# Cosformer attention followed by a leaky-ReLU feed-forward block on one core: a second order of the same steps, with other engines and ring places

## The chip, the cores and the metric

One core of a Trainium2 chip runs the program in one launch. The metric is the device time of one execution in microseconds (us). Five engines work side by side: TensorE (PE, with its weight loads as PEld), VectorE (DVE), ScalarE (ACT), GpSimd (POOL) and SyncE (SP), which here issues nearly all DMAs. Each engine runs its own instructions strictly in their order; between engines there are semaphores.

## The reference

```
r = max(x, 0); phi(x) = concat([r * cos_w, r * sin_w])         # head_dim 64 -> 128 features
kv  = einsum('bhsf,bhsd->bhfd', phi(k), v)                     # b 8, h 8, s 576, d 64
num = einsum('bhsf,bhfd->bhsd', phi(q), kv)
den = einsum('bhsf,bhf->bhs', phi(q), sum_s phi(k)) + 1e-6
x   = (num / den), heads side by side: 4608 tokens x 512
h   = x @ w_in                                                 # 512 x 2048
out = max(0.01 * h, h) @ w_out                                 # 2048 x 512, float32
```

All inputs and the output are float32 in DRAM; the matrix work is done in float16 with float32 sums.

## The kernel before, in words

The tokens are cut into nine groups of 512: groups 0 to 7 are the first 512 positions of the eight batches, group 8 gathers the 64 last positions of all eight. A group g passes through two halves.

**Attention half.** `lq`, `lk`, `lv` load q, k and v of a batch (L234, L244; L251 for group 8's q). `rq` and `rk` take the ReLU and round to float16 (L385 on ACT, L387 elsewhere). `kt` multiplies k by cosine or sine (L395, DVE), `v` copies v to float16, `kv` makes 72 small matmuls that contract over 64 rows (L444), `ko` copies their sums out. `q` multiplies q by cosine or sine (L408 ACT, L410 POOL, L414 DVE). `qT` turns two of a group's four q tiles by a DMA transposition on SP (L488). `n g.j` multiplies the turned q tile j with kv (8 matmuls, L544), `N g.j` divides (three DVE instructions, L555, L559, L560) and writes x. When all four are there, `xT g` turns the whole x of the group by one DMA transposition on SP (L500).

**Feed-forward half.** Groups 0 and 1 do it plainly (`f` L624, `e` L633, group 0's `F` L647 and store L662). From group 2 on, the first product is a 2x2 block scheme with seven products instead of eight (`f g.u.n`, four matmuls of 128x256 each, L763; u counts four column blocks). It needs sums of blocks of x, `X g.1` to `X g.4` (L677). The products are combined in four PSUM banks that are used in turn: `b`, `s` and `u` copy a bank on ACT or DVE (L420, L422), `y` and `z` add on DVE (L677), and `a`, `c`, `e`, `d` apply the leaky ReLU on ACT (L787). The second product is made the same way from group 1 on: `S g.n` are sums of blocks of the activations (L677, DVE), `F g.n.tt.h` the products (four matmuls of 128x256 each, L846), `M` and `O` take the sums out of PSUM, `D` stores them (L904 and L909; L895 for the last pieces). `W` and `T` make the sums of the weights once (L677). `cw` and `w` cast the weights as they arrive, and `i` are idle matmuls on a tile of zeros (L295) that fill the time before there is work.

**What sets the order.** No scheduler does: a string `ORDER` (from L31) names every step once, and the loop below emits them in this order. A step may carry the engine that does it (`:D` DVE, `:A` ACT, `:P` POOL) and the place in a ring of buffers that it takes (`@0` to `@3`). What a step is, is the same in both kernels; a step's instructions go to the end of their engine's queue, so the string fixes each engine's order, and a step that waits holds up everything behind it on its engine.

```
    for token in ORDER.split():
        token, *places[:] = token.split("@")
        name, _, e = token.partition(":")
        f, args = steps.pop(name)
        f(*args, *([engines[e]] if e else []))
```

A transposition is one DMA instruction on SP:

```
    def x_transpose_dma(g):
        nc.sync.dma_start_transpose(
            out=xT_tile(g).rearrange("p j c t -> p (j c) t"),
            in_=st["xs", g].rearrange("p j h d -> p (j h d)"),
        )
```

Of the kernel before, what the change touches and what calls it, by code (L numbers as in the profile page):

```python
# [37 lines left out]
xo0.1.0:A f0.1.c f0.2.c f0.3.a f0.1.b f0.3.c N0.1.1 cw.2:P cw.3:P xo0.0.1:D Lw1.5 f0.0.b xt0.1.1@0
f0.0.d f0.2.d f0.3.d f0.0.c Lw1.7 Lw1.8 xo0.1.1:D f0.3.e f0.4.a f0.0.e f0.2.e e0.1 cw.4:D f0.4.d
f0.1.d f0.1.e cw.8:D cw.5:D f0.5.a f0.5.d Lw1.6 Lq1@3 rq1.1:D rq1.0:D cw.7:P e0.0 f0.6.a@0 f0.6.d  # L40
f0.7.a q1.3.0:D q1.1.1:D f0.7.d Lw2.0@2 e0.2 q1.0.0:D q1.2.1:D q1.0.1:D q1.2.0:D w0.0:D Lk1.0 w0.2:D
cw.6:P e0.3 Lw2.1@1 q1.3.1:P f0.12@1 w1.0:P f0.13 rk1.0:D W1.1:D W0.1:D f0.14@0 f0.15 kt1.0.0 e0.6
f0.8@1 f0.9 e0.7 f0.10@0 f0.11 q1.1.0:A e0.4 qt1.3@1 qo1.3:A e0.5 F0.2.0 F0.3.0 F0.0.0@0 F0.3.2
qt1.2@1 F0.2.2 F0.1.0@1 F0.0.2 qt1.0@0 qo1.2:D qt1.1@1 w1.2:A Lv1.0 Lk1.1 v1.0:P qo1.0:D qo1.1:D
kt1.0.1 F0.0.4 F0.1.2 F0.0.6 F0.3.4 F0.3.6 kv1.0@1 F0.1.4 rk1.1:A kt1.1.0 F0.1.6 Lw2.2@0 Lw2.3.0
w2.0:D ko1.0:A n1.1.0@1 F0.2.4 F0.2.6 kt1.1.1 w2.2:A w3.0:A N1.1.0 F0.2.8 F0.3.8 n1.0.0@0 N1.0.0
F0.0.8 F0.3.10 F0.3.12 Lw2.3.2 w3.2:D F0.0.10 F0.2.10 F0.2.12 xt1.0.0@0 F0.2.14 Lv1.1 v1.1:A kv1.1@1
ko1.1:A lq2@3 rq2.0:P rq2.1:A F0.3.14 T1 q2.0.1:P q2.3.0:P O0.2:D@0 lk2@1 lv2.0@2 F0.0.12 n1.0.1@1
q2.2.1:P F0.0.14 O0.0:A@3 O0.3:D@1 n1.1.1 F0.1.8 F0.1.10 N1.0.1 xt1.1.0@1 xt1.0.1@0 F0.1.12 N1.1.1
xo1.0.1:D xo1.0.0:A q2.2.0:A q2.1.1:A F0.1.14 xo1.1.0:D xt1.1.1@0 q2.1.0:D q2.0.0:D xo1.1.1:A f1.4.0  # L50
f1.0.0@1 f1.1.0 f1.1.2 f1.5.0 f1.0.2 rk2.1:A v2.0:A f1.5.2 rk2.0:P kt2.0.0 kt2.1.1 kt2.0.1 q2.3.1:A
f1.4.2 f1.2.0@0 e1.0 e1.2 lv2.1 f1.3.0 W0.2:D kt2.1.0 T2 T3 f1.3.2 f1.2.2 T4 lk3@0 v2.1:P W0.4:D
f1.10@1 kv2 f1.11 e1.1 f1.6@0 rk3.1:A ko2:A qT2.0 e1.5 rk3.0:A n2.0 f1.7 N2.0 qT2.1 f1.12@1 kt3.0.0
f1.13 n2.1 lq3@2 e1.3 f1.8@0 rq3.1:P f1.9 lv3.0@3 O0.1:A@2 lv3.1 kt3.1.0 N2.1 e1.6 n2.2 f1.14@1
kt3.1.1 e1.4 N2.2 f1.15 rq3.0:A e1.7 n2.3 F1.1.0.0@0 F1.2.0.0@1 lq4@1 D0.1 kt3.0.1 N2.3 F1.2.1.0
F1.1.1.0 S1.1a S1.1b F1.1.1.1 F1.2.0.1 q3.2.0:D S1.1c F1.1.0.1 S1.2a F1.2.1.1 v3.0:A q3.1.0:A
q3.3.1:P q3.0.1:P q3.2.1:P v3.1:A kv3 M1.1:A S1.2b S1.2c F1.6.0.0@0 F1.6.1.0 F1.6.1.1 q3.3.0:A
q3.1.1:D S1.3c F1.6.0.1 O1.2@2 F1.5.0.0@1 xT2 S1.3a W0.3:D X2.1:D f2.0.1 S1.4b X2.2:D X2.3:D
F1.5.0.1 F1.5.1.0 f2.0.5 q3.0.0:A rq4.0:A ko3:A b2.0:A s2.0:A f2.0.6 M1.6 X2.4:P S1.3b f2.0.2 f2.1.1
D0.2 qT3.1 qT3.0 u2.0:D f2.0.3 F1.7.0.0 f2.0.7 rq4.1:A a2.0 z2.0 e2.0 F1.7.1.0 F1.7.1.1 f2.1.5 y2.0  # L60
b2.1:A S1.4a q4.0.0:A s2.1:A q4.1.0:D lv4.0@2 lv4.1 lk4@3 q4.2.1:P f2.0.4 c2.0 F1.5.1.1 n3.0 f2.1.6
D0.3 D1.2 q4.3.0:P q4.0.1:P D0.0 u2.1:A q4.1.1:A d2.0 f2.1.2 W1.2:P F1.7.0.1 f2.1.3 a2.1 W1.4:P
W1.3:P N3.0 lq5@0 f2.1.7 n3.1 f2.2.1 v4.1:P rk4.0:P M1.7 z2.1 F1.4.1.0 F1.4.0.0 rk4.1:P y2.1 f2.2.5
f2.1.4 e2.1 b2.2:A c2.1 f2.2.2 s2.2:A N3.1 n3.2 f2.2.6 q4.3.1:A d2.1 u2.2:A O1.5@0 v4.0:A f2.2.3
F1.3.1.0 F1.3.1.1 f2.2.7 N3.2 z2.2 n3.3 f2.3.1 F1.4.1.1 F1.4.0.1 F1.3.0.0 N3.3 y2.2 O1.4@1 e2.2
kt4.0.0 kt4.0.1 kt4.1.0 b2.3:A q4.2.0:A F1.3.0.1 f2.3.6 F2.1.0.0@0 a2.2 f2.3.5 u2.3:A c2.2 s2.3:A
f2.3.7 f2.2.4 F2.1.1.0 d2.2 f2.3.2 f2.3.3 y2.3 c2.3 a2.3 xT3 kt4.1.1 S2.1a z2.3 O1.3@2 qT4.0 X3.1:P
X3.2:P f2.3.4 d2.3 e2.3 kv4 f3.0.1 b3.0:A f3.0.5 F2.1.0.1 F2.1.1.1 f3.0.6 X3.3:D S2.1b S2.3b f3.0.2
M2.1:A ko4:A s3.0:D F2.2.0.0 f3.0.3 f3.1.1 n4.0 u3.0:A f3.0.7 F2.2.0.1 F2.2.1.0 F2.2.1.1 a3.0 S2.2a
S2.1c S2.3c S2.2c z3.0 e3.0 F2.6.0.0@1 b3.1:A rq5.1:A F2.6.1.0 f3.1.6 f3.1.2 N4.0 O2.2:D@3 S2.2b  # L70
y3.0 n4.1 u3.1:A lk5@2 rk5.0:P F2.6.1.1 f3.1.5 rq5.0:P q5.0.1:P q5.0.0:A X3.4:P qT4.1 D1.3 lv5.0@1
c3.0 rk5.1:A s3.1:A F2.5.0.0@0 f3.1.7 F2.5.1.0 F2.6.0.1 f3.0.4 N4.1 kt5.0.0 f3.1.3 D1.5 D2.2 lq6@3
# [6 lines left out]
f3.3.4 e3.3 O2.4@3 lk6@2 F2.3.1.1 b4.0:A f4.0.6 f4.0.2 N5.0 n5.1 F3.1.0.0@1 D2.5 s4.0:A c3.3 d3.3
q6.0.1:D q6.0.0:D S3.1b F3.1.1.0 F3.1.1.1 f4.0.3 u4.0:A O2.3@0 X4.3:D S3.2b f4.0.7 lq7@0 a4.0 S3.1c  # L80
f4.1.5 f4.1.1 F3.1.0.1 F3.6.0.0@0 N5.1 z4.0 D2.4 rk6.0:A e4.0 F3.6.1.0 S3.3c S3.2c b4.1:A qT5.1
F3.6.0.1 F3.6.1.1 f4.1.2 rq7.0:P q6.2.0:P q6.2.1:P rq7.1:P q6.3.0:P y4.0 M3.1:D X4.4:D n5.2 f4.1.6
F3.2.1.0 F3.2.1.1 rk6.1:A q6.1.1:A s4.1:A a4.1 u4.1:A c4.0 q6.3.1:A f4.1.3 f4.0.4 f4.1.7 F3.2.0.0
N5.2 M3.6 S3.3b z4.1 y4.1 d4.0 lv6.0@1 n5.3 F3.2.0.1 f4.2.1 F3.7.1.0 F3.7.0.0 F3.7.0.1 f4.2.5
F3.7.1.1 e4.1 b4.2:A N5.3 O3.2:A@3 kt6.0.0 kt6.1.1 v6.0:D kt6.0.1 D2.3 s4.2:A f4.2.6 f4.1.4 lv6.1
c4.1 qT6.0 f4.2.3 F3.5.0.0@1 F3.5.1.0 f4.2.2 v6.1:A u4.2:A M3.7 F3.5.0.1 f4.2.7 z4.2 d4.1 a4.2 e4.2
S3.4b y4.2 F3.4.0.0 f4.3.5 s4.3:D lq8.1@3 rq8.1:P xT5 f4.3.1 X5.1:P q7.0.1:P q7.0.0:A b4.3:A
F3.5.1.1 kt6.1.0 S3.4a F3.4.1.0 F3.4.1.1 f4.2.4 f4.3.6 f4.3.3 F3.4.0.1 f4.3.2 qT6.1 D3.2 d4.2 c4.2
u4.3:A a4.3 q7.1.1:A O3.5@0 q7.3.1:D z4.3 X5.2:P kv6 F3.3.1.0 f5.0.1 f4.3.7 f5.0.5 F3.3.0.0 lk7@2
O3.4@2 X5.3:D S4.1a y4.3 S4.3a e4.3 ko6:A n6.0 f4.3.4 b5.0:A f5.0.6 F4.1.0.0@0 D3.5 F4.1.1.0 lv7.0@1  # L90
# [1026 lines left out]
```

## Time and profile before

| what | value |
|---|---|
| time, three runs | 277.46 us median (276.22, 277.46, 277.86) |
| the profiled execution's own time | 278.54 us |
| its span, first to last instruction | 276.7 us, granted TensorE clock 0.994 |
| DMA traffic | 57.62 MB, HBM read 36.70 MB, written 9.44 MB |
| busy share of the 16 DMA queues' engines, 0 to 160 us | 0.90 to 1.12 in each 20 us |
| the same, 200 to 260 us | 0.23, 0.33, 0.12 |
| DMA transpositions on SP | 14 of q (median 5.1 us from issue to landing), 7 of x (5.0 us) |

The page of a profile gives each engine's busy time, and the chain of work that ended last. The view of waits names, for each engine, what ended its idle time. In a view in order of time a row has the start in us, the length in us, the engine (SPq is SP's sequencer while it issues a DMA), the line, what is written and read with the shapes, and in brackets the idle time before it with what ended it. Matmuls are pipelined: a group of four of 128x256 is shown 0.60 us long, but the next group starts 0.44 us after it.

### The profile page before, as it was taken

To read this page: it belongs to the slowest core of one execution; us is meant where nothing else is said; L and a number is where in the kernel's file an instruction comes from. 1 tells how busy PE (TensorE), PEld (TensorE's weight loads), DVE (VectorE), ACT (ScalarE), POOL (GpSimd) and SP (SyncE) were. 2 spreads that over 40 slices of the span, in tenths; PEclk is the share of its full clock that TensorE was granted. 3 is DMA by queue.
4 is the path that set the end of the run, shared out by engine and by line. 5 is a ranking of instruction groups with operands and counts; after the bars stand their busy time and mean duration, and the time that the engine had idled before them with its cause. 6 is when DMAs were issued, how large, how long until landed. Compare 5 with 4: busy or idle time off the path is not lost.

```text
span 276.7 us, 7179 instructions
## 1 busy us (share of the span) xinstructions
PE 263.6 (95%) x2942; PEld 222.3 (80%) x2942; DVE 222.0 (80%) x433; ACT 173.8 (63%) x278; POOL 81.4 (29%) x86
## 2 busy tenths in 40 slices
PE   8699999999989999997999999999999999999992
PEld 3366555555888999997999899999998999999981
DVE  4673797798989899999997899999688868867652
ACT  6645644898958977785787576665447636475300
...
GB/s 220 360 357 388 401 406 374 357 195 372 221 196 357 232 233 199 378 207 320 260 221 212 347 124 154 5 207 128 159 152 2 0 121 111 39 39 11 30 25 206
DMA packets 77265, 57.62 MB, mean 208 GB/s; under 512 B 49456, under 2 KB 65840, under 8 KB 76848
## 3 DMA queue, kind: packets, MB, share of 16 engines
...
q10 hardware_dynamic: 608, 0.52, 0.7%
q8 instruction: 23, 0.38, 0.6%
...
HBM read 36.70 MB, written 9.44 MB: 167 GB/s over the span
## 4 chain that ended last, share of the span: by engine, by line
PE 68%; DMA 14%; DVE 11%; issue 3%; SPq 1%; ACT 1%; POOL 1%; DVEq 0%; ACTq 0%
PE ps L846 27%; PE ps_f L763 26%; DMA qst<-in_q_dram 6%; PE ps_h L624 5%; DMA xT<-xs 5%; PE ps_o L647 4%; PE ps_kv L444 2%; PE ps_num L544 2%; DMA w1st<-in_moe_w_in_dram 2%; DVE qp L414 2%; DVE ext L677 1%; DMA out_dram<-osb 1%; DVE y L677 1%; DVE g L677 1%; DVE xs L560 1%
## 5 line engine op out<-in xcount | busy, mean ns | idle before, releaser
L787 ACT ACTIVATE g<-ps_f 128x512 f16<-128x512 f32 x84 | 48.9, 599 | 35.0 <-PE ps_f L763 20.2
L846 PEld LDWEIGHTS <-g 128*128 128x128 f16 x640 | 61.7, 98 | 6.5
L846 PE MATMUL ps<-w,g 128*128 128x256 f16 x496 | 65.3, 273 | 0.0
L763 PEld LDWEIGHTS <-w 128*128 128x128 f16 x448 | 48.7, 113 | 4.3 <-issue 3.5
L763 PE MATMUL ps_f<-xT,w 128*128 128x256 f16 x336 | 49.3, 273 | 2.2 <-DMA xT<-xs 2.2
L763 PEld LDWEIGHTS <-wext 128*128 128x128 f16 x336 | 36.7, 114 | 0.6
L846 PE MATMUL ps<-T,ext 128*128 128x256 f16 x240 | 32.6, 273 | 0.0
L624 PE MATMUL ps_h<-xT,w 128*128 128x512 f16 (+1 forms) x144 | 29.2, 356 | 0.2 <-ACT xT L420 0.2
L846 PEld LDWEIGHTS <-ext 128*128 128x128 f16 x256 | 24.8, 98 | 2.6
L763 PE MATMUL ps_f<-X,wext 128*128 128x256 f16 x176 | 26.3, 273 | 0.0
L624 PEld LDWEIGHTS <-w 128*128 128x128 f16 x144 | 15.7, 114 | 10.4
L677 DVE TENSOR_TENSOR ps_f<-ps_f,u 128x512 f32<-128x512 f32 x28 | 19.4, 694 | 4.8 <-PE ps_f L763 3.5
L677 DVE TENSOR_TENSOR y<-ps_f,s 128x512 f32<-128x512 f32 x28 | 19.1, 683 | 3.7 <-PE ps_f L763 3.5
L633 ACT ACTIVATE g<-ps_h 128x1024 f16<-128x1024 f32 x16 | 16.0, 1023 | 7.5 <-PE ps_h L624 7.3
L787 ACT ACTIVATE g<-y 128x512 f16<-128x512 f32 x28 | 17.8, 634 | 3.8 <-DVE y L677 3.8
L560 DVE TENSOR_TENSOR xs<-ps_num,rden 128x512 f16<-128x512 f32 x28 | 19.3, 691 | 1.0
L395 DVE TENSOR_TENSOR kp<-kst,ang 128x1152 f16<-128x1152 f16 x24 | 18.8, 805 | 0.7 <-ACT kst L385 0.7
L420 ACT COPY ps_f<-ps_f 128x512 f32<-128x512 f32 x25 | 14.3, 573 | 5.9 <-PE ps_f L763 5.3
L763 PE MATMUL ps_f<-X,w 128*128 128x256 f16 x112 | 16.9, 273 | 0.7 <-DVE y L677 0.4
L846 PE MATMUL ps<-ext,g 128*128 128x256 f16 x128 | 17.4, 273 | 0.0
L677 DVE TENSOR_TENSOR osb<-ps,ext 128x512 f32<-128x512 f32 x23 | 15.7, 682 | 2.0 <-PE ps L846 2.0
L763 PE MATMUL ps_f<-xT,wext 128*128 128x256 f16 x112 | 16.8, 272 | 0.0
...
## 6 DMA issues: line engine op xcount, KB each, us to landing
...
qst<-in_q_dram SPq DMA_DIRECT2D x7, 1024.0 KB, 10.6
...
```

The costliest lines, as they stand in the source:

```text
L395: nc.vector.tensor_tensor(out=st["kp", b][:, lo:hi, :, f * D : (f + 1) * D].rearrange("p c j (x y) -> p (c j) x y", y=2), in0=halved("k", ...
L414: eng.tensor_scalar(out=o, in0=i, scalar1=0.0, scalar2=col, op0=ALU.max, op1=ALU.mult)
L420: nc.scalar.copy(o, i)
L444: nc.tensor.matmul(ps[:, o, (c - lo) * NE : (c - lo + 1) * NE], lhsT=st["kp", b][sl, c, j, :], rhs=vm[sl, c, j, :], start=(j == 0), stop=( ...
L560: nc.vector.tensor_tensor(out=xs, in0=ps[:, :, 0 : 4 * NE].rearrange("p a (b e) -> p a b e", e=NE)[:, :, :, 0:D], in1=rden.rearrange("p (a ...
L624: nc.tensor.matmul(ps[:, m % 2, lo:hi], lhsT=w1[m // 4, c][0][:, w1[m // 4, c][1], m % 4 : 512 : 4], rhs=xT[:, lo // P : hi // P, c, :], s ...
L633: nc.scalar.activation(g_tile(g)[:, 2 * i : 2 * i + 2, :], st["h", g, i], AF.Lrelu)
L647: nc.tensor.matmul(st["ps_o", g, tt], lhsT=st["g", g][:, m, tt * P : (tt + 1) * P], rhs=w2[:, m, :], start=(m == 0), stop=(m == NFT - 1),)
L677: eng.tensor_tensor(out=o, in0=a, in1=b, op=op)
L763: nc.tensor.matmul(ps[:, mi * HT : (mi + 1) * HT], lhsT=a[:, c, 2 * r0 + mi : 512 : 4], rhs=b[:, c], start=(n in (1, 5) and mi == 0 and c ...
L787: nc.scalar.activation(g_tile(g)[:, m : m + 2, r * HT : (r + 1) * HT], {"a": A, "c": y22, "e": E, "d": B_}[e].rearrange("p (m t) -> p m t" ...
L846: nc.tensor.matmul(ps[:, tt], lhsT=a[:, i, tt * P : (tt + 1) * P], rhs=b[:, i], start=(first and i == 0), stop=(i == NPR - 1 and (apart or ...
```

## The change

Only the string `ORDER` is replaced. Every step that stood in it still stands in it once, so the number of matmuls (2942), of DMAs and of sums is the same. What differs is the order, the letter of the engine on some steps, and the ring places.

The string's first lines, a place around the transposition of x of group 4, and its end, of some 100 lines each:

```diff
-i.10@1 i.13@0 Lq0.0@3 rq0.0:A qt0.1.0@1 i.11@0 Lk0.0@0 Lq0.1 i.14@1 i.7@1 qt0.0.0@0 i.4@1 rq0.1:A
-qt0.0.1 rk0.0:P kt0.0.0 Lk0.3 kt0.0.1 rk0.3:D kt0.3.0 Lk0.1 rk0.1:D kt0.1.1 kt0.1.0 Lv0.0@1 i.6@1
...
-q5.3.1:D f3.3.3 kv5 F2.4.1.0 ko5:A d3.2 xT4 f3.3.6 F2.4.0.1 f3.3.2 n5.0 F2.4.1.1 rq6.0:P q5.3.0:P
-u3.3:A f3.3.7 z3.3 X4.1:D S3.2a f4.0.1 F2.3.0.0 F2.3.0.1 y3.3 q6.1.0:P X4.2:P a3.3 F2.3.1.0 f4.0.5
...
-F8.3.1.1 O8.5.0@0 F8.4.0.1 F8.4.1.1 O8.3.1@1 D8.5.1 O8.2:A@3 D8.2 D7.4 D7.3 F8.3.0.0 D8.3.1 D8.5.0
-F8.3.0.1 O8.4@2 D8.4 O8.3.0@3 D8.3.0
+Lk0.0@1 Lq0.0@2 i.14@0 rq0.0:P rk0.0:P qt0.0.0@1 qt0.1.0@0 i.12@0 qo0.0.0:A Lk0.2 kt0.0.0 kt0.0.1
+rk0.2:D i.3@1 i.5@1 i.2@1 Lq0.1 Lk0.1 qo0.1.0:A rq0.1:P rk0.1:A i.7@1 Lk0.3 Lv0.0@0 qt0.0.1 i.1@0
...
+kt5.1.1 lq6@1 u3.3:A c3.2 f3.3.3 f3.3.2 F3.1.0.0@1 f3.3.7 v5.0:P v5.1:P q5.1.0:P kv5 y3.3 z3.3 a3.3
+d3.2 xT4 f3.3.4 F3.1.1.0 F2.3.1.0 c3.3 S3.1a S3.2a F2.3.1.1 d3.3 e3.3 F3.1.0.1 F2.3.0.1 f4.0.1
...
+F8.2.1.0 F8.2.1.1 M8.7 F8.4.1.0 O8.2:A@2 O8.5.1@1 D7.5 D7.3 S8.4b S8.4a F8.4.1.1 F8.5.0.0 F8.5.0.1
+F8.3.1.0 F8.3.1.1 F8.4.0.0 F8.4.0.1 O8.5.0@3 O8.3.1@0 D8.5.1 D8.2 F8.3.0.0 F8.3.0.1 D8.5.0 D8.3.1
+O8.4@1 D8.4 O8.3.0@2 D8.3.0
```

**What PE finds between a group's last `n` and its first `f`.** The transposition of x lies between the two. Counted from the two strings, PE has these steps to do meanwhile (4x256 stands for a step of four matmuls of 128x256):

| group | before | after |
|---|---|---|
| 2 | 13 of 4x256, kv | 14 of 4x256, kv |
| 3 | 14, kv | 16, kv |
| 4 | 15, kv, n | 16, kv |
| 5 | 27, kv | 17, kv |
| 6 | 30, kv, n | 16, kv, n |
| 7 | 38, n of group 8 | 19, n of group 8 |
| 8 | 26 | 20 |

**Engines.** These steps change sides most (before, after): `s` on DVE 9, 6; `u` on DVE 10, 6; `b` on DVE 3, 0 (the rest of each 28 on ACT). The ReLU of batch 0's q, `rq0`, moves from ACT to POOL. `W1.3` moves from POOL to DVE. DVE has 410 rows of instructions before and 396 after, ACT 272 and 285, POOL 83 and 80, SP 92 and 88 (equal neighbours count as one row).

**SP around the transposition of x of group 4** (`xT` in a row is that transposition; `qpT` one of q, `kst`, `vst`, `qst` loads, `out_dram` stores). Before:

```order
L234 DMA qst<-in_q_dram 128x8x256
L244 DMA vst<-in_v_dram 128x2x576
L488 DMA_TRANSPOSE qpT<-qp 128x16x128
L904 DMA out_dram<-osb 128x2x256
L500 DMA_TRANSPOSE xT<-xs 128x16x128
L244 DMA kst<-in_k_dram 128x4x576
```

After:

```order
L488 DMA_TRANSPOSE qpT<-qp 128x16x128
L244 DMA vst<-in_v_dram 128x2x576
L662 DMA out_dram<-osb 128x512
L244 DMA vst<-in_v_dram 128x2x576
L904 DMA out_dram<-osb 128x2x256
L234 DMA qst<-in_q_dram 128x8x256
L500 DMA_TRANSPOSE xT<-xs 128x16x128
L904 DMA out_dram<-osb 128x2x256
L488 DMA_TRANSPOSE qpT<-qp 128x16x128 x2
```

The transposition of q that stood two places ahead of group 4's x now stands two places behind it (with a second one), and loads and stores stand ahead of it.

**DVE ahead of the division of group 2's last tile** (its three rows are `den`, `rden`, `xs`; the `ext` rows are sums of group 1's activations). Before:

```order
L560 TENSOR_TENSOR xs<-ps_num,rden 128x512
L395 TENSOR_TENSOR kp<-kst,ang 128x18x64
L555 TENSOR_SCALAR den<-ps_num 128x8
L559 RECIPROCAL rden<-den 128x8
L560 TENSOR_TENSOR xs<-ps_num,rden 128x512
```

After:

```order
L560 TENSOR_TENSOR xs<-ps_num,rden 128x512
L414 TENSOR_SCALAR qp<-qst,sin_t 128x8x64
L677 TENSOR_TENSOR ext<-g 128x512
L677 TENSOR_TENSOR ext<-ext,g 128x1024
L555 TENSOR_SCALAR den<-ps_num 128x8
L559 RECIPROCAL rden<-den 128x8
L560 TENSOR_TENSOR xs<-ps_num,rden 128x512
```

One multiplication of k between the last two divisions has become one of q and two sums.

**POOL at the sums of the first weight** (`wext` and `w_3_0_104` are such sums, `W1.2`, `W1.4`, `W1.3`). Before:

```order
L677 TENSOR_TENSOR X_175<-xT,X_174 128x512
L410 TENSOR_SCALAR qp<-qst,sin_t 128x8x64
L410 TENSOR_SCALAR qp<-qst,cos_t 128x8x64
L410 TENSOR_SCALAR qp<-qst,sin_t 128x8x64
L677 TENSOR_TENSOR wext<-wext,w_2_0_102 128x1024
L677 TENSOR_TENSOR wext<-w_2_2_103,wext 128x1024
L677 TENSOR_TENSOR w_3_0_104<-w_2_0_102,w_3_0_104 128x1024
```

After:

```order
L677 TENSOR_TENSOR X_175<-xT,X_174 128x512
L677 TENSOR_TENSOR wext<-w_2_2_103,wext 128x1024
L387 TENSOR_SCALAR qst<-qst 128x16x64
L410 TENSOR_SCALAR qp<-qst,cos_t 128x8x64 x2
```

Of three such sums in a row one is left here; the first stands further up on POOL, and the third has moved to DVE.

More of the change, by code (lines that the diff above doesn't have):

```diff
@@ L38 @@
[L38 to L72, printed above, removed]
@@ L79 @@
[L79 to L90, printed above, removed]
```

142 lines of the change are left out of this document (94 added, 48 removed).

## The prediction

> **What bounds the kernel now.** I read the page first, then the table of busy time by stage, then PE's waits, and last the timeline around the longest of them.
>
> ```profile
> PE 263.6 (95%) x2942; PEld 222.3 (80%) x2942; DVE 222.0 (80%) x433; ACT 173.8 (63%) x278; POOL 81.4 (29%) x86
> ```
>
> PE is busy for 263.6 us, 95% of the span. The change alters no matmul, so it can win only what PE waits, and the two ends. That caps the gain at a few per cent.
>
> ```profile
> 80.00:100.00 20.00, 19.70 (x261) 18.30 (x260) 18.70 (x33) 17.61 (x32) 13.08 (x11) 1.00 1.05 269
> 100.00:120.00 20.00, 19.72 (x214) 18.53 (x207) 19.48 (x37) 15.47 (x27) 9.84 (x9) 1.00 1.12 258
> 120.00:140.00 20.00, 18.59 (x253) 17.20 (x251) 19.69 (x38) 14.49 (x26) 10.64 (x10) 1.00 1.07 292
> 200.00:220.00 20.00, 20.00 (x208) 18.63 (x207) 16.56 (x35) 12.56 (x23) 2.32 (x2) 1.00 0.23 53
> ```
>
> Here the columns after the length are PE, PEld, DVE, ACT, POOL, the granted clock, the DMA share and GB/s. From 80 to 140 us DVE is as full as PE (57.9 of 60 us) and the DMAs are full too; at 200 us PE waits for nothing and DVE has 3 us to spare.
>
> ```profile
> PE ps_f L763 <- DMA xT<-xs: 2.2, 2, 1.4
> PE ps_qt L520 <- ACT r L385: 1.6, 1, 1.6
> PE ps_qt L510 <- DVE qpT L422: 0.5, 1, 0.5
> PE ps_f L763 <- DVE y L677: 0.4, 1, 0.4
> PE ps_num L544 <- DVE xs L560: 0.3, 1, 0.3
> PE ps_f L763 <- POOL X L677: 0.3, 1, 0.3
> PE ps_numh L579 <- DVE osb L422: 0.3, 1, 0.3
> ```
>
> Two waits for a transposition of x (groups 2 and 4) make 2.2 us; five small ones after the first 20 us make 1.8 us. A group of four matmuls is shown 0.60 us long though the next starts 0.44 us after it, so each wait really costs 0.16 us more: 2.2 + 0.3 = 2.5 us, and 1.8 + 0.8 = 2.6 us. Together 5.1 us can be won in the middle.
>
> **The change part by part.** First the transposition of x. The longest wait, of group 4:
>
> ```profile
> 116.31 0.42 PE L544 MATMUL ps_num<-kv,qpT 128*128 128x66 f16 x8
> 116.57 0.60 PE L846 MATMUL ps<-w,g 128*128 128x256 f16 x4
> 117.00 0.60 PE L763 MATMUL ps_f<-X1b,wext 128*128 128x256 f16 x4
> ...
> 120.06 0.60 PE L763 MATMUL ps_f<-xT,wext 128*128 128x256 f16 x4
> 120.59 1.46 PE L444 MATMUL ps_kv<-vm,kp 64*128 64x66 f16 x72
> 121.98 0.61 PE L846 MATMUL ps<-ext,g 128*128 128x256 f16 x4
> ...
> 126.44 0.60 PE L763 MATMUL ps_f<-xT,w 128*128 128x256 f16 x4 [1.41 <-DMA xT<-xs]
> ```
>
> ```profile
> 117.21 0.69 DVE L560 TENSOR_TENSOR xs<-ps_num,rden 128x512 f16<-128x512 f32 x1
> ```
>
> ```profile
> 115.02 4.47 SPq L488 DMA_TRANSPOSE qpT<-qp  x1
> 119.53 0.57 SPq L904 DMA_DIRECT2D out_dram<-osb  x1
> 120.21 2.89 SPq L500 DMA_TRANSPOSE xT<-xs  x1
> ```
>
> ```profile
> L500 SPq DMA_TRANSPOSE xT<-xs x7: 2380/3035/3149, 70.8 to 223.3; - x7
> DMA to landing us min/median/max: 4.6/5.0/6.6
> ```
>
> The last quotient matmuls give PE back at 116.57. The division ends at 117.90 (1.33 us later), but SP is held by a transposition of q until 119.49 and by a store, so x is issued at 120.21 (2.31 us lost) and PE goes on at 126.44 (6.23 us after the issue). That is 9.87 us from end to use. PE had 15 steps of 0.44, a kv of 1.39 and an n of 0.26, some 8.2 to 8.3 us, and waited for the rest. With SP free the same path takes 1.33 + 4.6 to 6.6, say 6.0 to 8.0 us.
>
> The new order gives PE, by the counts of steps in the table of the change: group 2 14 x 0.437 + 1.39 = 7.5 us (before 7.1), group 3 8.4 (7.5), group 4 8.4 (8.3), group 5 8.8 (13.2), group 6 8.6 (14.8), group 7 8.8 (17), group 8 8.7 (11.4). So it evens them out just above the 8.0 us. For group 4 no transposition of q stands directly ahead on SP any more, and DVE has three 0.69 us rows between the last two divisions, which fit into the 3.3 us that PE spends between those tiles. I keep 0.2 us of its 1.57 us wait: gain 1.4, bounds 0.1 (it needs 9.87 again, against 8.4) and 1.57. For group 2 the need was 8.0 us (a landing of 6.6 us); its division now stands behind three DVE rows (a q product and two sums) instead of one k product, and the time to use grows by 0.44. I take a wait of 0.3: gain 0.7 of 0.97, bounds 0 and 0.97. Sum **-2.1 us**.
>
> Groups 5 to 8 lose their cushion of 3 to 8 us. At 6.0 to 8.0 us needed they still wait for nothing; at 9.87 each waits 1.1 to 1.3 us. After 160 us the DMAs are at half load or less, so short landings are likelier; DVE may divide late. I take **+0.6 us** for the four together, bounds 0 and 4.7.
>
> Second, DVE and POOL in the full stage.
>
> ```profile
> 83.12 2.57 POOL L677 TENSOR_TENSOR wext<-wext,w 128x1024 f16<-128x1024 f16 x1
> 83.62 2.22 DVE L414 TENSOR_SCALAR qp<-qst,cos_t 128x512 f16<-128x512 f16 x1
> 85.76 0.15 DVE L555 TENSOR_SCALAR den<-ps_num 128x8 f32<-128x8 f32 x1
> 86.93 0.43 PE L544 MATMUL ps_num<-kv,qpT 128*128 128x66 f16 x8 [0.29 <-DVE xs L560]
> ```
>
> ```profile
> L414 DVE TENSOR_SCALAR qp<-qst,sin_t x4: 340/344/352, 73.9 to 152.4; 128x512 f16<-128x512 f16 x4
> ```
>
> A q product that takes 0.344 us alone took 2.22 us and ended with POOL's weight sum; the division behind it came late, and PE waited 0.29 (really 0.45) us. In the new order only one of these three sums stands at this place. The Trainium skill, page "SBUF — State Buffer", section "Who interferes with whom", says that DVE and GpSimd share a port pair and whoever issues first keeps it for the whole instruction while the other fully blocks; this trace agrees (2.22 us against 0.344). By that rule alone the one sum left can still block a q product, the wait of 0.45 us would stay, and the sum below would be -1.7 instead of -2.15.
>
> ```profile
> L560 DVE TENSOR_TENSOR xs<-ps_num,rden 128x512 f16<-128x512 f32 x28 | 19.3, 691 | 1.0
> L395 DVE TENSOR_TENSOR kp<-kst,ang 128x1152 f16<-128x1152 f16 x24 | 18.8, 805 | 0.7 <-ACT kst L385 0.7
> L422 DVE COPY u<-ps_f 128x512 f32<-128x512 f32 x10 | 6.9, 686 | 1.5 <-PE ps_f L763 1.1 <-ACT s L420 0.3
> L420 ACT COPY u<-ps_f 128x512 f32<-128x512 f32 x18 | 10.6, 589 | 6.6 <-PE ps_f L763 6.6
> ```
>
> Ten bank copies (`b`, `s`, `u`) go from DVE (686 ns) to ACT (589): DVE loses 6.9 us of work, ACT gains 5.9 of a spare 100. Most of it lies after 140 us, though. In the full stage the relief is that the attention half of a group is done later: its four divisions (0.69 us each) and four k products (0.81) are 6 us of DVE for one group, and n of groups 5 and 6 stand some 8 us of PE work further down, a quarter of a group's 36 us, so about 1.5 us of DVE leaves the stage. The five small waits of 2.6 us all hang on DVE or POOL; other places will now be the tightest, so I take **-1.0 us**, bounds -2.6 (all gone) and +0.3.
>
> Third, the head.
>
> ```profile
> 4.91 1.06 ACT L385 ACTIVATE r<-qst 128x1024 f16<-128x1024 f32 x1
> ...
> 5.82 0.67 POOL L387 TENSOR_SCALAR r<-kst 128x576 f16<-128x576 f32 x1 [3.95 <-DMA kst<-in_k_dram]
> ...
> 9.05 1.06 ACT L385 ACTIVATE r<-qst 128x1024 f16<-128x1024 f32 x1 [3.08 <-DMA qst<-in_q_dram]
> ...
> 10.15 0.64 PE L520 MATMUL ps_qt<-r 128*64 128x128 f16 x16 [1.57 <-ACT r L385]
> ```
>
> ```profile
> L387 POOL TENSOR_SCALAR qst<-qst 128x1024 f16<-128x1024 f32 x6 | 7.3, 1216 | 26.3 <-DMA qst<-in_q_dram 14.9 <-DVE xs L560 11.3
> ```
>
> The first half of q came at 4.9 and the first k at 5.8. The new order loads that k first, and a second k ahead of the second half of q, which then comes one k piece later (some 0.8 us) and is rectified on POOL in 1.22 instead of 1.06 us: the wait that ended at 10.15 ends near 11.1. The last v piece comes no later than before, so part is made up: **+0.65 us**, bounds 0 and +1.0.
>
> Last, the tail.
>
> ```profile
> 271.76 0.42 DVE L677 TENSOR_TENSOR osb<-ps_f,ext 128x256 f32<-128x256 f32 x1 [0.52 <-DMA out_dram<-osb]
> ```
>
> The last result waited 0.52 us for its buffer to be stored. The new order makes that buffer's result (`O8.2`) some 2 us earlier: **-0.3 us**, bounds 0 and -0.5.
>
> Sum: -2.1 + 0.6 - 1.0 + 0.65 - 0.3 = -2.15 us, 278.54 to 276.4 us for an execution like the profiled one. That one is 1.1 us above the median of the three runs; from the median it is 277.46 - 2.15 = **275.3 us**, 0.8% less. Own range of this case 273.7 to 277.1.
>
> One price is left out of the sum. Ahead of kv, which works on 64 rows of the array, the next start comes 0.53 us after 120.06 instead of 0.44: a change of the array's form costs 0.09 us. The new order has 34 such changes instead of 36, both in the head, where idle matmuls fill the room anyway. The Trainium skill, page "TensorEngine Tiling (Array Packing)", section "Key Properties", says that a change of the tiling mode drains the TensorE; the trace agrees, with these 0.09 us, and by the rule the sum would be -2.35.
>
> **The rivals.** (1) *All goes.* The order closes every wait after 20 us, and nothing new opens: -5.1 - 0.3 + 0.65 = -4.75, 272.7 us. For it: the distances of 8.4 to 8.8 us all sit just above what an undisturbed transposition needs. Against: DVE stays full from 80 to 140 us.
>
> (2) *DVE keeps the beat.* In the full stage PE's 1.57 us at group 4 was time in which DVE worked on (19.69 of 20 us). If DVE is the bound there, PE starts earlier and then waits for divisions and bank sums instead. Then only the 1.5 us that leave DVE's stage and the tail's 0.3 are won, against the head's 0.65 and the late groups' 0.6: about -0.5, 277.0 us. For it: the busy time. Against: PE's own waits for DVE there are short (0.3 to 0.4 us).
>
> (3) *Slower: late transpositions.* If x is issued as late in the new order as in group 4 (9.87 us from end to use), groups 4 to 8 wait 1.5 + 1.1 + 1.3 + 1.1 + 1.2 = 6.2 us. Against that stand the old 1.57 of group 4, 0.44 at group 2, 1.0 of the small waits and 0.3 of the tail; with the head: 6.2 - 3.3 + 0.65 = +3.5, 281.0 us. It decides from the point where end to use passes 8.4 to 8.8 us. For it: the cushions of 3 to 8 us are cut for four groups, and a held SP alone cost group 4 its 2.3 us. Against: transpositions of q no longer stand directly ahead of groups 4 and 5, and DVE has room after 140 us.
>
> **How the numbers follow.** Chances: the forecast 0.50, all goes 0.18, DVE keeps the beat 0.20, slower 0.12. About 1%, 2.8 us, is what a measurement of this kernel tells from no change. Below 274.7 us lie all of (1) but 0.02 and 0.22 of the forecast's 0.50: faster 0.38. Within 1% lie 0.28 of the forecast, 0.02 of (1) and 0.19 of (2): same 0.49. Slower: (3) and 0.01 of (2), 0.13. The range 272.6 to 278.4 takes in (1), the forecast and (2) and leaves out most of (3).
>
> **What would show it.** Right: PE's waits name the transposition of x with under 1 us; end to use is under 8.8 us in groups 4 to 8; the first feed-forward matmul (18.08 us before) comes 0.3 to 1.0 us later; DVE busy near 214 us; PE's last matmul some 2 us earlier. Wrong: a wait for x of over 1 us in groups 5 to 8 (rival 3), PE waits for DVE of more than 2.6 us between 80 and 140 us (rival 2), or a head that loses over 1.5 us.

## The result and the profile after

The changed kernel takes 274.74 us (median of 4 runs, 273.90 to 275.48) against 277.66 us for the kernel before (4 runs, 276.22 to 278.50): ratio 0.990, 95% interval 0.986 to 0.994. The forecast was 275.3 us. The time is right; several of the terms behind it are not, and they are told apart below. The profiled execution took 273.9 us, with a span of 271.9 us at a granted clock of 1.000. Of the kernels below one, `a_q_ahead_x`, has its profile from a slower execution (granted clock 0.948), so its rows show the order of events only.

The page after, its busy line and its chain of waits by engine:

```profile
PE 264.6 (97%) x2942; PEld 222.5 (82%) x2942; DVE 210.1 (77%) x419; ACT 182.2 (67%) x292; POOL 79.7 (29%) x86
...
PE 92%; DVE 3%; POOL 1%; ACT 1%; issue 0%; DVEq 0%
```

PE's work is the same (264.6 against 263.6 us), but its share rises to 97%, and 92% of the chain that ends last is PE itself. DVE is at 210.1 us; 214 was foretold.

The table of busy time by stage, in the same stretches as before (columns as there):

```profile
80.00:100.00 20.00, 19.96 (x263) 18.46 (x262) 18.55 (x35) 14.80 (x27) 11.63 (x12) 1.00 0.91 230
100.00:120.00 20.00, 20.00 (x208) 18.96 (x207) 18.94 (x40) 16.39 (x28) 6.22 (x7) 1.00 1.02 278
120.00:140.00 20.00, 20.00 (x262) 18.79 (x261) 17.73 (x37) 16.37 (x30) 3.64 (x5) 1.00 1.05 252
```

From 80 to 140 us PE goes from 58.0 to 59.96 of 60 us, and DVE from 57.9 to 55.2. The DMAs are nearly as full as before (shares of 0.91 to 1.05, before 1.05 to 1.12). What PE waits for in the whole span is now three lines of the view of waits, all of them in the first 20 us:

```profile
PE ps_idle L295 <- DVE blank L290: 1.2, 1, 1.2
PE ps_numh L579 <- ACT kv L420: 0.6, 2, 0.5
PE ps_xth L599 <- DVE xs L560: 0.4, 2, 0.2
```

The waits for the transposition of x (2.2 us) and the small ones on DVE and POOL are gone. To see where the time went I cut each span at two matmuls that all the kernels have: `F0.2.0`, the first of ff2 of expert 0 (line 647), and the last one of the kernel (its end is modelled by the profile). The middle lies between them; the tail is from that end to the end of the span. The kernels named here are those of the experiments.

| kernel | first ff1 matmul, us | `F0.2.0`, us | middle, us | tail, us |
|---|---|---|---|---|
| before | 18.08 | 33.42 | 237.96 | 5.3 |
| three variants of the old order (`b_...`) | 16.69 to 16.95 | 32.30 to 32.56 | 238.9 to 242.0 | 4.8 to 5.4 |
| after | 19.42 | 33.78 | 233.88 | 4.2 |
| the new order once more (`a_again`) | 19.52 | 33.88 | 234.68 | 4.2 |
| new order, idle matmuls left out (`a_no_idle`) | 18.01 | 33.38 | 235.08 | 4.3 |
| new order, old head (`a_head_b`) | 16.76 | 33.30 | 233.88 | 4.2 |
| the same, `q1.0.0` later (`c_head_q`) | 16.87 | 33.91 | 233.87 | 4.2 |
| the same, `w0.0` earlier too (`c_head_qw`) | 17.08 | 33.45 | 233.88 | 4.2 |
| old head, w2 loaded first (`c_head_load`) | 16.95 | 33.31 | 233.89 | 4.2 |

Between the two profiled executions the head costs 0.36 us by `F0.2.0`, the middle wins 4.08 and the tail 1.07: 4.8 us of span. The medians differ by only 2.9. The table tells why: the profiled execution of before had its head 0.9 to 1.1 us later than the three variants that share that head, and a second profile of the new order has a middle 0.8 us longer (most of it the transposition of x, below). With these two the sum is +1.4 - 3.3 - 1.1 = -3.0 us, close to the difference of the medians. That pairing was made after the fact and from single profiles, so it shows that the figures are consistent, not where each of the medians got its time.

The cut is not quite fair to the two orders. The old one has eight turns of q (L510, 32.98 to 33.42 us in the profile of before) ahead of `F0.2.0`, the new one has them behind it. For equal work the head costs 0.4 us more than the table says, and the middle wins 0.4 more.

**The transposition of x, group 4.** PE, DVE and SP after, in order of time:

```profile
117.82 0.42 PE L544 MATMUL ps_num<-kv,qpT 128*128 128x66 f16 x8
118.08 0.60 PE L763 MATMUL ps_f<-xT,w 128*128 128x256 f16 x4
...
126.44 0.60 PE L763 MATMUL ps_f<-xT,w 128*128 128x256 f16 x4
```

```profile
119.14 0.69 DVE L560 TENSOR_TENSOR xs<-ps_num,rden 128x512 f16<-128x512 f32 x1
```

```profile
119.89 2.84 SPq L500 DMA_TRANSPOSE xT<-xs  x1
...
123.54 3.42 SPq L488 DMA_TRANSPOSE qpT<-qp  x1
```

The division still comes late on DVE (it ends at 119.83, 1.75 us after the quotient matmuls), but SP is free and issues x 0.06 us later instead of 2.31 us. The transposition of q now stands behind it and a store. Of the 8.36 us that PE works between the two (8.4 were counted), 1.81 go to the issue, and the landing has 6.55. All seven transpositions of x (the landings are a row of the same view):

```profile
L500 SPq DMA_TRANSPOSE xT<-xs x7: 1762/1906/2962, 71.4 to 219.4; - x7
...
DMA to landing us min/median/max: 4.3/4.9/6.1
```

With at most 6.1 us from issue to landing, x lands 0.7 to 2.6 us ahead of its use in every group. The reserve is thin, as the second profile of the new order shows (line 500, then PE's wait for it):

```profile
DMA to landing us min/median/max: 4.6/6.0/7.2
```

```profile
PE ps_f L763 <- DMA xT<-xs: 0.5, 1, 0.5
```

Here the same transpositions take up to 7.2 us; group 5 waits 0.5 us at 150.70. Between these two executions of one order the landing of one group varies by up to 1.9 us (group 4: 4.3 and 6.2).

At group 2 SP was never held: before, x was issued 0.03 us after its division. There the wait of 0.81 us went mostly because the landing took 4.6 us (issue at 71.40) instead of 6.6. It takes 6.1 to 6.6 us in the four kept profiles of the old order, but in those of the new order 4.3 to 4.7 in seven and 6.0 to 6.1 in three. What decides between the two is open.

**The tail.** The last result, `O8.3.0`, after:

```profile
267.75 0.42 DVE L677 TENSOR_TENSOR osb<-ps_f,ext 128x256 f32<-128x256 f32 x1 [0.24 <-PE ps_f L846]
268.26 0.56 SPq L895 DMA_DIRECT2D out_dram<-osb  x1
268.31 0.79 ACTq L895 DMA_DIRECT2D out_dram<-osb  x1
```

It waits for PE and no longer for a buffer: 0.51 us from PE's last end to the result instead of 0.80. From there to the end of the span it takes 3.73 us instead of 4.52. The result is stored in two pieces, one issued by SP and one by ACT. The later of the two is now issued 0.14 us after the result. Before, it came 1.12 us after it (the result ended at 272.18):

```profile
273.30 0.47 SPq L895 DMA_DIRECT2D out_dram<-osb  x1
```

That piece landed faster, though, 1.97 us after its issue against 2.55 for the last one now, so the last landing comes 2.68 us after the result instead of 3.09.

### The profile page after: what moved, and what is told of

The parts are those of the page before. It is cut to its first block, busy times and chain, and to the rows that moved or that the text cites. A ratio compares the mean times of both kernels' runs of the same rounds, so it can differ in the third digit from the quotient of the medians.

```text
span 271.9 us, 7170 instructions
## 1 busy us (share of the span) xinstructions
PE 264.6 (97%) x2942; PEld 222.5 (82%) x2942; DVE 210.1 (77%) x419; ACT 182.2 (67%) x292; POOL 79.7 (29%) x86
## 4 chain that ended last, share of the span: by engine, by line
PE 92%; DVE 3%; POOL 1%; ACT 1%; issue 0%; DVEq 0%
PE ps L846 35%; PE ps_f L763 32%; PE ps_h L624 8%; PE ps_o L647 5%; PE ps_idle L295 4%; PE ps_kv L444 3%; PE ps_num L544 3%; POOL vm L422 1%; PE ps_f L846 1%; PE ps_qt L520 1%; DVE kp L395 1%; DVE xs L560 1%; PE ps_qt L510 1%; PE ps_numh L579 0%; DVE T L677 0%
## 5 line engine op out<-in xcount | busy, mean ns | idle before, releaser
L763 PE MATMUL ps_f<-xT,w 128*128 128x256 f16 x336 | 48.7, 273 | 0.0
L420 ACT COPY u<-ps_f 128x512 f32<-128x512 f32 x22 | 12.9, 587 | 13.5 <-PE ps_f L763 13.4
L420 ACT COPY ps_f<-ps_f 128x512 f32<-128x512 f32 x28 | 16.1, 575 | 5.0 <-PE ps_f L763 4.3
L422 POOL CAST vm<-vst 128x1152 f16<-128x1152 f32 (+1 forms) x10 | 14.3, 1431 | 16.6 <-DMA vst<-in_v_dram 11.5
L395 DVE TENSOR_TENSOR kp<-kst,ang 128x1152 f16<-128x1152 f16 x24 | 17.7, 766 | 0.2 <-ACT kst L385 0.2
```

Of the source, the lines that this page charges most:

```text
L395: nc.vector.tensor_tensor(out=st["kp", b][:, lo:hi, :, f * D : (f + 1) * D].rearrange("p c j (x y) -> p (c j) x y", y=2), in0=halved("k", ...
L420: nc.scalar.copy(o, i)
L422: eng.tensor_copy(o, i)
L763: nc.tensor.matmul(ps[:, mi * HT : (mi + 1) * HT], lhsT=a[:, c, 2 * r0 + mi : 512 : 4], rhs=b[:, c], start=(n in (1, 5) and mi == 0 and c ...
```

## The experiments

Diffs show the steps of `ORDER`; the rest of each kernel is unchanged.

**Free SP in the old order.** In the kernel before, the transposition of q goes behind x of group 4, with the `n` that needs it:

```diff
-F2.7.1.0 qT5.0 D1.4 ... xT4 f3.3.6 F2.4.0.1 f3.3.2 n5.0 F2.4.1.1 ... f4.0.6 f4.0.2
+F2.7.1.0 D1.4 ... xT4 qT5.0 f3.3.6 F2.4.0.1 f3.3.2 F2.4.1.1 ... f4.0.6 n5.0 f4.0.2
```

> The kernel before, with one transposition of q (qT5.0) put behind the transposition of x of group 4 on SP instead of ahead of it, and its first use (n5.0) seven PE steps further down so that it does not wait itself. Theory A (SP held by the transposition of q cost group 4 its wait): x of group 4 is issued within 0.1 us of the last division instead of 2.31 us after it, PE's wait of 1.41 us there falls below 0.3, and the whole is 1.0 to 1.6 us faster (ratio near 0.995). Theory B (DVE is the bound from 80 to 140 us and keeps the beat): the wait there falls just the same, but PE waits for DVE rows further down grow by about as much, and the time changes by less than 0.4 us.

277.87 us against the kernel before: ratio 1.000 (0.997 to 1.003). SP and PE of this kernel:

```profile
117.53 3.00 SPq L500 DMA_TRANSPOSE xT<-xs  x1
```

```profile
122.74 0.60 PE L763 MATMUL ps_f<-xT,w 128*128 128x256 f16 x4
...
127.90 0.60 PE L763 MATMUL ps_f<-X,wext 128*128 128x256 f16 x4 [0.54 <-POOL X L677]
...
129.98 0.20 PE L544 MATMUL ps_num<-kv,qpT 128*128 128x66 f16 x1 [0.78 <-DVE xs L560]
```

x is issued at 117.53 and lands at 121.89; its matmul at 122.74 waits for nothing. But the next ones wait, for a sum on POOL and for a division on DVE, and nothing is won. Freeing SP at this place was worth nothing in the old order, where DVE and POOL were next in line: my rival 2, for this one edit. (The second wait stands at an `n` of group 5, which this edit itself moved, so part of it is the edit's own.)

**Hold SP in the new order.** The mirror image: `qT5.0` goes directly ahead of `xT4` in the changed kernel.

```diff
-d3.2 xT4 f3.3.4 F3.1.1.0 ... f4.0.6 qT5.0 qT5.1
+d3.2 qT5.0 xT4 f3.3.4 F3.1.1.0 ... f4.0.6 qT5.1
```

> The kernel after, with qT5.0 put directly ahead of the transposition of x of group 4 on SP, as it stood before. Theory A: SP is held for 2 to 4 us when the division ends, x lands 2 to 4 us later than in the kernel after (3.2 to 4 us of it over the 2.2 us that the landing stood ahead of the use), so PE waits 0.5 to 2.5 us at group 4's first feed-forward step and the time grows by 0.5 to 2.5 us over the kernel after. Theory B: DVE uses the pause to run ahead, later waits are none to begin with, so the loss stays too, but the kernel before's smaller waits do not come back. What tells them apart is the first run; this one prices a held SP in the new order.

276.50 us, ratio 0.995 (0.992 to 0.997), against 0.990 (0.986 to 0.994) for the new order: 1.8 us more by the medians, 1.3 by the ratios, and the intervals just overlap. SP and PE:

```profile
121.32 3.10 SPq L488 DMA_TRANSPOSE qpT<-qp  x1
124.51 1.82 SPq L500 DMA_TRANSPOSE xT<-xs  x1
```

```profile
129.99 0.60 PE L763 MATMUL ps_f<-xT,w 128*128 128x256 f16 x4 [1.23 <-DMA xT<-xs]
```

In this execution a transposition of q ahead of x holds it for 3.1 us, and PE waits 1.2. Where nothing else is next in line, a held SP costs about what the first term of the sum gave it for group 4 (1.4 us).

**The letters alone, both ways.** The 24 bank copies `b`, `s`, `u` whose engine differs: the new letters in the old order, and the old letters in the new.

```diff
-u2.1:A u2.2:A s3.0:D u3.2:A s4.3:D ... u8.1:D u8.3:D s8.3:A
+u2.1:D u2.2:D s3.0:A u3.2:D s4.3:A ... u8.1:A u8.3:A s8.3:D
```

> The order before with the engines of the bank copies of the new order, the same 24 letters the other way. Theory A: PE's waits for DVE and POOL after 20 us (1.8 us in the profile of before, 2.6 with the pipeline) fall by more than half and the time by 1 us or more. Theory B: under 0.5 us either way, since in the full stage from 80 to 140 us the new order even has four copies on DVE where the old one has three.

281.63 us, ratio 1.015 (1.011 to 1.020): slower by 4 us. Its stages and two of its waits:

```profile
80.00:100.00 20.00, 18.86 (x254) 17.39 (x252) 17.27 (x35) 15.59 (x28) 12.94 (x11) 1.00 1.04 269
100.00:120.00 20.00, 17.80 (x185) 16.60 (x184) 17.71 (x33) 14.31 (x24) 9.67 (x9) 1.00 1.10 258
```

```profile
116.98 0.60 PE L763 MATMUL ps_f<-xT,w 128*128 128x256 f16 x4 [1.85 <-DVE u L422]
...
158.66 0.60 PE L763 MATMUL ps_f<-xT,wext 128*128 128x256 f16 x4 [1.35 <-ACT s L420]
```

DVE fell by 10.4 us over the span (to 211.6), and from 80 to 120 us it has over 2 us to spare in each 20. PE waits all the same, for single copies that stand too far back on the engine that they were given to: the `u` starts on DVE at 116.24, behind a division and two products of k, and the `s` on ACT at 158.02, behind another copy and two activations. The other direction:

> The new order with the engines of the bank copies (b, s, u) of the order before: 24 letters differ, ten copies more on DVE in the end. Theory A (DVE's relief opened the middle): DVE is 7 us busier, PE waits again for DVE by 1.5 us or more, and the time grows by 1 to 3 us over the new order. Theory B (the places of the steps did it, the copies only fill room that DVE had): the time grows by less than 0.5 us.

284.79 us, ratio 1.027 (1.023 to 1.031): the new order loses 10 us and is worse than before. PE's longest waits there:

```profile
PE ps_num L544 <- DVE xs L560: 1.8, 1, 1.8
...
PE ps_f L763 <- ACT u L420: 1.0, 1, 1.0
PE ps_f L763 <- ACT s L420: 1.0, 1, 1.0
```

Neither theory foresaw a loss in both directions. Letters and places fit only each other: the relief of DVE is not a term that can be priced by itself. (Which of the 24 copies cost the most was not told apart.)

**`W1.3` back on POOL** in the new order:

```diff
-M1.6 W1.3:D S1.3b
+M1.6 W1.3:P S1.3b
```

> The new order with one weight sum (W1.3) back on POOL, where it takes 2.1 us instead of 0.7. Theory A (a long POOL sum blocks DVE's rows that share its port, and DVE is short of time there): one or two DVE rows near 74 us take 1 to 2 us longer, group 2's block sums come late, and PE waits 0.3 to 1.0 us; the time grows by as much. Theory B (DVE has room there since the copies and the attention rows moved): rows are blocked just the same, but PE waits less than 0.2 us and the time stays within 0.3 us.

275.77 us, ratio 0.994 (0.991 to 0.997): about 1.0 us over the new order, though the intervals overlap. POOL, DVE and PE:

```profile
71.24 2.12 POOL L677 TENSOR_TENSOR w<-w,w 128x1024 f16<-128x1024 f16 x1
```

```profile
71.41 2.24 DVE L677 TENSOR_TENSOR ext<-g 128x512 f16<-128x512 f16 x1
```

```profile
74.71 0.83 PE L846 MATMUL ps<-T,ext 128*128 128x256 f16 x6 [0.24 <-DVE ext L677]
77.18 1.47 PE L846 MATMUL ps<-w,g 128*128 128x256 f16 x12 [0.39 <-DVE ext L677]
```

The same DVE row in the new order, with nothing on POOL beside it:

```profile
71.29 0.42 DVE L677 TENSOR_TENSOR ext<-g 128x512 f16<-128x512 f16 x1
```

While POOL works on the sum for 2.12 us, one sum of activations on DVE takes 2.24 us instead of 0.42. The sums behind it come late, and PE waits for them twice, 3 to 6 us later.

**The tail in the old order.** Group 7's last two stores go ahead of a store of group 8:

```diff
-O8.3.1@1 D8.5.1 O8.2:A@3 D8.2 D7.4 D7.3 F8.3.0.0
+O8.3.1@1 D7.4 D7.3 D8.5.1 O8.2:A@3 D8.2 F8.3.0.0
```

> The kernel before, with the last two stores of group 7 put ahead of the last group's stores on SP. Theory A (these two stores of 256 KB, issued 3 us before the end, slow the last ones): the time from PE's last matmul to the end falls from 5.3 us to 4.3 to 4.7, and the whole is 0.5 to 1.0 us faster, without any other part of the change. Theory B (the tail of the new order is short because one result, O8.2, is copied out 2 us earlier and its buffer comes free): no change beyond 0.3 us, the last result still waits about 0.5 us for its buffer.

277.46 us, ratio 1.001 (0.998 to 1.005). In its profile the tail is 4.8 us instead of 5.3. The buffer's wait is gone (0.28 us), although its result `O8.2` is made where it was: its store landed in 2.9 us instead of 3.2. Behind the result (at 274.33) 0.25 us are won. The last stores:

```profile
274.52 0.53 SPq L895 DMA_DIRECT2D out_dram<-osb  x1
```

```profile
274.80 0.56 ACTq L895 DMA_DIRECT2D out_dram<-osb  x1
```

SP's piece is issued 0.19 us after the result, but ACT's only 0.47 us after it, and the last landing comes 2.89 us after it. The half us in all is too little for the comparison to tell, and a wait of 2.2 us for DVE's work at another place of the same execution shows how much the old middle varies.

**The head.** Seven steps of idle matmuls (they compute nothing of the result) are left out of the new order:

```diff
-qt0.0.1 i.1@0 i.15@0 i.10@0 i.11@0 rk0.3:D ... v0.1:D i.9@0 i.0@0 i.13@0 qt0.1.1@1
+qt0.0.1 rk0.3:D ... v0.1:D qt0.1.1@1
```

> The kernel after without seven idle matmuls that stand between the turns of q in the head (nothing of the computation is left out). In the kernel after they take 0.43 us each, 3.0 us in a row, and the sum over k behind them starts at 14.27 us though its operands are there near 12.3. Theory A (PE's own idle matmuls hold the head): that sum starts 1.5 to 2 us earlier, the first feed-forward matmul comes at 17.4 to 18.4 instead of 19.42, and the whole is 0.8 to 1.8 us faster. Theory B (the loads set the head): the last v lands at 13.0 and the weights' first block at 17.1 whatever PE does, so the first feed-forward steps wait for casts instead and the gain is below 0.4 us. A lower granted clock in the head would show as matmuls slower than 0.22 us each for 128x512.

274.04 us, ratio 0.986 (0.983 to 0.989). PE in the head of the changed kernel:

```profile
10.46 2.98 PE L295 MATMUL ps_idle<-blank 128*128 128x512 f16 x7
13.37 0.64 PE L520 MATMUL ps_qt<-r 128*64 128x128 f16 x16
...
14.27 0.74 PE L444 MATMUL ps_kv<-vm,kp 64*128 64x66 f16 x36
...
19.42 0.60 PE L624 MATMUL ps_h<-xT,w 128*128 128x256 f16 x4
```

Seven idle matmuls in a row take 2.91 us, 0.42 us each (each starts only after the one before it has ended; a 128x512 matmul of ff2, from 33.78 us, starts 0.22 us after the one before it), and push the last transposition of q and the first kv back. Without them the first ff1 matmul starts 1.4 us earlier, at 18.01, but `F0.2.0` only 0.4. The whole old head ahead of the new order (its first 97 steps, through `xo0.1.1`):

```diff
-Lk0.0@1 Lq0.0@2 i.14@0 rq0.0:P rk0.0:P ... xo0.1.1:D
+i.10@1 i.13@0 Lq0.0@3 rq0.0:A qt0.1.0@1 ... xo0.1.1:D
```

> The new order from the first feed-forward steps on, with the head of the order before in front of it (its first 97 steps, up to the last turn of group 0's x: loads, engines, idle matmuls and places of the kernel before). Theory A (the new head is a loss: in the profiles of the runs so far the first feed-forward matmul comes near 16.8 us with the old head and near 19.0 with the new one, 0.4 us of which is order): the whole is 1.2 to 2.0 us faster than the new order, 272.8 to 273.6 us, ratio near 0.983. Theory B (after the head the arrival of the second weight's blocks sets the pace, as it did without the idle matmuls, where 1.1 us won in the head left 0.7): the gain is 0 to 0.7 us.

273.72 us, ratio 0.987 (0.983 to 0.991). PE and ACT of this kernel:

```profile
31.15 1.89 PE L624 MATMUL ps_h<-xT,w 128*128 128x512 f16 x8 [1.06 <-ACT g L633]
33.30 2.32 PE L647 MATMUL ps_o<-w,g 128*128 128x512 f16 x10 [0.26 <-DVE w L422]
```

```profile
29.47 0.72 ACT L408 ACTIVATE qp<-r,cos_t 128x512 f16<-128x512 f16 x1 [1.67 <-DVE r L387]
```

ff1 starts 2.66 us earlier than in the changed kernel, yet `F0.2.0` only 0.48. One ACT instruction, `q1.0.0`, stands in the queue ahead of the activation that PE needs, and it waits 1.67 us for a load of q by way of DVE. So I moved it (first pair of lines), in a second kernel a weight cast as well (second pair), both from the old head with the new order, and ran the new order itself beside them.

```diff
-e0.6 w0.0:D q1.0.0:A kt1.0.1 ... e0.7 e0.4 w0.2:A
+e0.6 w0.0:D kt1.0.1 ... e0.7 e0.4 q1.0.0:A w0.2:A
...
-f0.7.d q1.1.1:D e0.0 ... e0.6 w0.0:D kt1.0.1
+f0.7.d e0.0 ... e0.6 w0.0:D q1.1.1:D kt1.0.1
```

> The new order unchanged, once more on this chip, to stand beside the next two: 0.990 of the kernel before (0.986 to 0.994). If the thin reserve of the new order mattered (landings 0.7 to 2.6 us ahead of their use), a second profile should show a wait for x in some group; the theory that the new places hold says none above 0.3 us, and the same seven idle matmuls of about 0.43 us each ahead of kv0.0.

> The new order with the old head and ACT's q1.0.0 moved behind e0.4. Theory (the head's gain of 2.2 to 2.5 us was given back at one ACT instruction that waited 1.67 us for DVE's r): the wait of f0.10 (1.06 us) goes and the time is about 1 us under the old head alone, 272.7 us, ratio 0.983. Rival (the gain is given back wherever the next late w2 weight or drain is): f0.10 starts on time but F0.2.0 or the rotary copies of group 1 wait for what was 1 us late, and the time stays at 273.7.

> The same with DVE's w0.0 ahead of its q1.1.1 as well. Theory: the wait of F0.2.0 for the DVE weight cast (0.3 to 0.4 us) goes too, 272.4 us. Rival: the cast waits for its load instead, or q1.1.1 is then late for the transpositions of q in group 1, and the time is as in the run above or longer.

On one chip: the new order 274.70 us, ratio 0.989 (0.984 to 0.993); with `q1.0.0` moved 273.64, ratio 0.985 (0.981 to 0.989); with both 274.05, ratio 0.986 (0.982 to 0.990). Against the old head alone (273.72, 0.987) neither wins anything that these runs can tell: the rival held. PE and DVE with `q1.0.0` alone moved:

```profile
33.91 2.32 PE L647 MATMUL ps_o<-w,g 128*128 128x512 f16 x10 [1.92 <-DVE w L422]
```

```profile
33.18 0.67 DVE L422 CAST w<-w2st 128x1024 f16<-128x1024 f32 x1
```

The wait moved whole from the activation to the first weight of ff2, which landed at 32.58 and was cast at 33.18. In the new order the loads stand as q, k, w2; in the old as q, w2, k. The last run puts w2's load first, in the kernel with `q1.0.0` alone moved:

```diff
-f0.0.e Lq1@3 Lk1.0 rq1.1:D rq1.0:D ... rk1.0:D kt1.0.0 ... f0.12@1 Lw2.0@0 ... w0.0:D
+f0.0.e Lw2.0@0 Lq1@3 Lk1.0 rq1.1:D rq1.0:D ... rk1.0:D w0.0:D kt1.0.0 ... f0.12@1
```

> Old head, q1.0.0 behind e0.4, and the load of the first w2 weight issued ahead of the loads of q and k for group 1 (the order change had put k's load ahead of it), with its DVE cast ahead of kt1.0.0. Theory (the landing of that load sets F0.2.0, the first matmul of ff2, whatever the head before it does: landings 31.2 to 32.6 us, F0.2.0 at 33.3 to 33.9 us in all five kernels with the new places): it lands near 30.7 us as in the old order, F0.2.0 starts at 32.1 to 32.3 us, when the matmuls ahead of it are done, and the time is 1.0 to 1.7 us under the run with the old head and q1.0.0 alone: 272.0 to 272.7 us, ratio about 0.980. Rival (the loads share one rate, and who is put back is late next): q and k of group 1 land 1.4 to 2.6 us later, the transpositions of q and the keys of group 1 or F0.0.x wait for them, and the time stays at 273.6 us or goes above it.

273.84 us, ratio 0.989 (0.984 to 0.994). SP, DVE and PE:

```profile
15.26 0.34 SPq L281 DMA_DIRECT2D w2st<-in_moe_w_out_dram  x1
17.53 0.37 SPq L234 DMA_DIRECT2D qst<-in_q_dram  x1
20.28 2.25 SPq L244 DMA_DIRECT2D wext<-in_k_dram  x1
```

```profile
30.55 1.30 DVE L387 TENSOR_SCALAR r<-qst 128x1024 f16<-128x1024 f32 x2 [5.03 <-DMA qst<-in_q_dram]
31.89 0.76 DVE L387 TENSOR_SCALAR r<-wext 128x1152 f16<-128x1152 f32 x1
32.57 0.69 DVE L422 CAST w<-w2st 128x1024 f16<-128x1024 f32 x1
```

```profile
33.31 2.32 PE L647 MATMUL ps_o<-w,g 128*128 128x512 f16 x10 [1.30 <-DVE w L422]
```

The weight is there at 27.49 us, 3.7 to 5.1 us earlier than in the other kernels with the new places, so the theory that its landing sets `F0.2.0` falls. Its cast stands on DVE behind the ReLUs of q and k, whose loads now land at 30.45 and 31.87, and starts where it did before. In the kernels with the new places, whichever load comes first, the cast starts after the last of the three has landed. The old order has its cast ahead of the ReLU of k: in `b_q_behind_x` it starts at 31.59 us, while k lands at 32.15, and `F0.2.0` follows at 32.32. So with the cast ahead of those ReLUs in the new places as well, `F0.2.0` might start when ff1 ends, near 32; that was not tried.

## Why the prediction was right, and which steps failed

1. *What bounds the kernel:* PE, with 5.1 us to be won in the middle. Right: the middle of the new order is 233.87 to 233.89 us in five kernels, 4.1 us under the profiled one of before, or 4.5 for equal work. Every listed wait went; the rest of the 5.1 is in pauses too short for the view of waits (in the trace after, matmuls at 48.95, 60.97, 80.28, 82.38 and 86.33 us start 0.1 to 0.3 us late, 0.9 us together; before, two such make 0.2). Rival 1 described the middle of this execution, though a second one kept 0.8 us.

2. *Transposition of x of groups 2 and 4, -2.1 us:* right in place and size; the waits of 2.5 us went. The counted distances held (8.36 us measured at group 4). The reason given for group 4, SP, is borne out in the new order (1.3 to 1.8 us when it is held again) and refuted as a sufficient cause in the old one, where freeing it won nothing. At group 2 the 0.44 us of more PE work would not have covered the wait; a landing that was 2 us shorter did, which was luck of the execution: with 6.1 us in the second profile x came just in time (0.04 us).

3. *Groups 5 to 8, +0.6 us:* too dear in one execution (no wait), nearly right in the other (0.5 us at group 5). Rival 3's danger is real but small: the longest landings were 6.1 and 7.2 us, and the case behind 281 us needed an issue as late as the old group 4's. With SP free the issue followed the division by 0.03 to 0.06 us. Shorter landings after 160 us, which I gave as a reason, did not come clearly (4.7 to 5.9 us, against 4.3 to 6.1 ahead of that), and the load there was misread: the DMA share before is 0.44, 0.76 and 0.23 in the stretches from 160 to 220 us, not half or less throughout.

4. *DVE and POOL in the full stage, -1.0 us:* this is the step that failed. The waits went altogether, so the term was mis-sized; more than that, its reasoning by busy time was wrong. I counted ten copies and a stage's worth of attention that leave DVE. The letters alone give the old order that relief and make it 1.5% slower, and from 80 to 126 us three `u` in fact go to DVE against one `s` to ACT. What wins is the joint choice of place and engine for each step: taking the 24 letters back costs 10 us, one `W1.3` about 1.0. In the new order no product of q stands beside a weight sum: the longest one on DVE (1.27 us) stands beside POOL's cast of v, and PE waits for neither. So the wait of 0.45 us that the rule of the Trainium skill (page "SBUF — State Buffer", section "Who interferes with whom") would have left did not come. The block itself is real: with `W1.3` on POOL a DVE row took 2.24 us instead of 0.42.

5. *Head, +0.65 us:* the size is about right by `F0.2.0` (0.36 against the profiled execution, some 1.4 against the other profiles of that head), but not the cause. q's second half did not come late (8.58 us after, 9.02 before; 7.74 in the second profile of the new order, 7.64 and 7.82 in two variants of the old). Seven idle matmuls of 0.42 us delay kv, and ff1 starts 1.34 us later than before (0.3 to 1.0 was the sign given for it), 2.5 to 2.7 than in the variants. Most of this is no loss, since `F0.2.0` waits for loads and DVE's casts of group 1 until 33.3 to 33.9 us in every kernel with the new places, whatever the head does.

6. *Tail, -0.3 us:* right in size for the buffer (0.28 us), but its reason is not shown: in the old order the same wait went with group 7's two stores out of the way, without `O8.2` being earlier. And the tail won 1.1. The other 0.8 lies behind the result, and I had not counted it. Half of it, 0.4 us, is up to the last landing, where the last stores are issued 1.0 us sooner; group 7's late stores account for 0.2 of that by the experiment in the old order. The other 0.4 is between the last landing and the end of the span (1.46 us before, 1.04 after); its cause stays open.

7. *The sum:* -2.15 against -2.9 us in the medians and -4.8 between the profiled executions. Terms 4 and 6 gave more and the head took more, so the total came out close: that these errors offset each other is luck. Between the profiled executions they do not, and the last matmul ends 3.7 us earlier, not some 2. I set the sum against the median because the profiled execution was 1.1 us over it; that execution's late head bears this out.

A version slightly better than both: the new order with the old head, 273.6 to 274.1 us in four kernels, against 274.7 for the new order. About 0.3%; the intervals overlap, so this is likely rather than shown.
